# One core of attention and feed-forward: v staged in float32, w_out in long rows, transposes by head

## The chip, the cores and the metric

The kernel runs on one NeuronCore of a Trainium2 chip. The core has TensorE for matmuls (PE in the profile; PEld is its weight load), VectorE (DVE), ScalarE (ACT), GpSimd (POOL) and SyncE (SP), which work side by side and wait for one another by semaphores. SP and GpSimd issue most of the DMA transfers. The metric is the device time of one execution in microseconds (us); lower is better.

## The reference

Attention with a relative position bias is computed for 8 batches of 8 heads, 576 tokens, 64 values a head. Its output, 4608 tokens of 512 values, then goes through two dense layers with a leaky ReLU between.

```python
scores = q @ k.T / sqrt(64) + bias_table[bucket(|i - j|)]   # per batch and head, 576 x 576
attn   = softmax(scores)
x      = (attn @ v) -> 4608 x 512
h      = x @ w_in                       # 512 -> 2048
out    = maximum(0.01 * h, h) @ w_out   # 2048 -> 512
```

All inputs and the output are float32 in DRAM. The kernel works in bfloat16 inside.

## The kernel before

**Attention.** The heads are taken in pairs: 4 pairs a batch, 32 pairs in all, numbered 0 to 31. For a pair, q and k (96 rows of 6 x 64 values a head) are first brought into one row for both heads (`rows`, L385), transposed by TensorE into PSUM (`turn_by_pe`, L395) or, from pair 10, by DMA, and copied to SBUF as `qt` and `kt` (L407). `apart` (L411) adds a block in which the last 64 tokens of both heads stand apart. Six score units a pair follow (`score`, L432 to L440): units 0 to 3 each give 128 keys by 512 queries of both heads, units 4 and 5 the rest. ScalarE takes the exponential of each (L446, L448, L453) into the tile `at` (for pair 2 the tile `extra`), and VectorE multiplies the band near the diagonal by the exponential of the bias (`band`, L465), which comes from the tile `hk` (and `hk4` for the last 64 keys). `av` (L480, L482) multiplies with v, 25 matmuls a head; v lies in `vn` (512 tokens) and `v4` (the last 64), with a column of ones that gives the row sums. VectorE divides (L491, L492) into `opair`, and TensorE (L506, copied by VectorE at L510) or a DMA turns it into `xT`.

**Feed-forward.** Nine tiles T of 512 tokens. For each, 16 in-products of four matmuls (`ffn_in`, L523), each followed by a leaky ReLU on ScalarE (L528) into `gt`; then 4 groups of 16 matmuls (`ffn_out`, L535), a copy to SBUF (L540) and a store. Tile 0 needs the four pairs of batch 0; tile 1 needs batch 1 as well.

**Order.** The order of every engine is written by a planner (`Plan`): each step has an engine, a cost, the steps it needs and a rank; the planner plays them through and emits them in that order, so that on the chip every engine runs its list strictly in order. PSUM buffers are counted too (two for scores, one for `av`, a pool of three for the rest). While the plan is before its first feed-forward step, TensorE's planned idle time is filled with matmuls on a tile of zeros, `junk` (L712).

**Loads.** The float32 q and k of the first pair come by SP and ScalarE. GpSimd issues the loads that cast to bfloat16 on the way: q and k of the other pairs (L195, two or four heads a DMA), v of batch 1 (L225, L230) and later batches (L203, L209), the halves of w_in (L351) and of w_out (L357). The v of batch 0 is loaded by SP uncast into the tile `first` (L312, L314), behind the row of the bias (L308) and the loads of `hk` (L318, L325). GpSimd casts it into `vn` and `v4` (`cast_v`, L333, L336), after it has waited for all of it to issue the first half of w_in (`gate`, L339):

```python
pool_load(("w_in", 0), 1.0, lambda: (gate(vraw4[SL : SL + 1, 0, 0:1], SL), load_w_in(0)), WH, after=[vrt])
vc = [add("POOL", 0.6, [vrt] + prev, lambda c=c: cast_v(c), 0) for c in range(NJ + 1)]
```

The tile `first` shares two buffers of 16 KB a partition with `extra` and with the `gt` of the feed-forward tiles.

Of the kernel before, what the change touches and what calls it, by code (L numbers as in the profile page):

```python
# [36 lines left out]
class Plan:  # L37


    LAG = 0.25  # L40

    def __init__(self, slots):
        self.tasks = []
        self.slots = {k: [0.0] * v for k, v in slots.items()}

# [14 lines left out]
    def order(self):  # L60
# [4 lines left out]
        first = False  # L65
        while any(waiting.values()):
# [35 lines left out]
            if t["rank"] >= 10000 and e == "PE" and not first:  # L102
                first = True
                self.slots["M"].append(r)
                t["first"] = True
# [3 lines left out]
    def run(self, fill):  # L109

        fills = True
        for t in self.order():
            if t.get("first"):
                fills = False
# [8 lines left out]
def kernel(  # L123
# [17 lines left out]
    P = 128  # L141
# [72 lines left out]
    def load_v(b, h0, h1, by_head):  # L214
        i = b % NBUF
        p0, p1 = h0 // 2, h1 // 2
        if by_head:
            for h in range(h0, h1):
                nc.gpsimd.dma_start(
                    out=vn[i][:, :, h, 0:D],  # L220
                    in_=v[b, h, 0 : NJ * P, :].rearrange("(c s) d -> s c d", s=P),
                )
        else:
            for c in range(NJ):
                nc.gpsimd.dma_start(  # L225
                    out=vn[i][:, c, h0:h1, 0:D],
                    in_=v[b, h0:h1, c * P : (c + 1) * P, :].rearrange("h s d -> s h d"),
                )
        for e in range(2):
            nc.gpsimd.dma_start(  # L230
                out=v4[i][e * SL : (e + 1) * SL, p0:p1, e, 0:D],
                in_=v[b, h0 + e : h1 : 2, NJ * P : S, :].rearrange("h s d -> s h d"),
            )
# [18 lines left out]
    vraw_sb = first[:, qk_e : qk_e + NJ * H * D].rearrange("p (c h d) -> p c h d", c=NJ, h=H)  # L252
    vraw4 = first[:, qk_e + NJ * H * D : qk_e + (NJ * H + n_pairs) * D].rearrange("p (h d) -> p h d", h=n_pairs)
    extra = gt_pool.tile([P, n_fc, TT], BF16, name="extra", tag="gt").rearrange("p f t -> p (f t)")
    spare = extra[:, 0 : ATW + SL], extra[:, ATW + SL : ATW + SL + S + SL]
# [5 lines left out]
    load_qk(0, 2, 4)  # L261
    load_qk(0, 4, 6)
# [22 lines left out]
    clear_v(nc.gpsimd, 0)  # L285
    for i in range(3):
        clear_edges(nc.gpsimd, i)
    clear_v(nc.gpsimd, 1)
# [21 lines left out]
    def load_v_raw():  # L310
        for c in range(NJ):
            nc.sync.dma_start(out=vraw_sb[:, c, :, :], in_=v[0, :, c * P : (c + 1) * P, :].rearrange("h s d -> s h d"))  # L312
        for e in range(2):
            nc.sync.dma_start(out=vraw4[e * SL : (e + 1) * SL, :, :],  # L314
                                in_=v[0, e::2, NJ * P : S, :].rearrange("h s d -> s h d"))

# [13 lines left out]
    def cast_v(c):  # L330

        if c < NJ:
            nc.gpsimd.tensor_copy(out=vn[0][:, c, :, 0:D], in_=vraw_sb[:, c, :, :])  # L333
            return
        for e in range(2):
            nc.gpsimd.tensor_copy(out=v4[0][e * SL : (e + 1) * SL, :, e, 0:D], in_=vraw4[e * SL : (e + 1) * SL, :, :])  # L336

    def gate(t, row=0):
        nc.gpsimd.tensor_copy(out=w_in_sb[row : row + 1, 0, 0:1], in_=t)  # L339

# [11 lines left out]

    def load_w_out(half):
        if half > 1:
            return
        n = n_fc // 2
        nc.gpsimd.dma_start(  # L357
            out=w_out_sb[:, half * n : (half + 1) * n, :],
            in_=moe_w_out[half * n * P : (half + 1) * n * P, :].rearrange("(f p) e -> p f e", p=P),
        )  # L360


# [28 lines left out]

    def turn_by_pe(n, j):
        ps = turned[n, j] = ps_m_pool.tile([P, 8 * P], BF16, name="ps_t", tag="m")
        for c in range(NC):
            nc.tensor.transpose(ps[:, c * RQ : (c + 1) * RQ], in_=prs[n][0:RQ, j, c, :],  # L395
                                identity=ident[0:RQ, 0:RQ])
# [118 lines left out]
    def ffn_in(T, f0):  # L515
        t0, w = tiles[T]
        if f0 == 0:
            gts[T] = gt_pool.tile([P, n_fc, TT], BF16, name="gt", tag="gt")
        pm = pms[T, f0] = ps_m_pool.tile([P, TT], FP32, name="pm1", tag="m")
        for j in range(TT // w):  # L520
            f = f0 + j
            for c in range(n_cc):
                nc.tensor.matmul(pm[:, j * w : (j + 1) * w], lhsT=w_in_sb[:, c, f * P : (f + 1) * P],  # L523
                                 rhs=xT[c][:, t0 : t0 + w], start=(c == 0), stop=(c == n_cc - 1))

    def ffn_act(T, f0):
        t0, w = tiles[T]
        nc.scalar.activation(gts[T][:, f0 : f0 + TT // w, 0:w], pms.pop((T, f0)).rearrange("p (j t) -> p j t", t=w),  # L528
                             AF.Prelu, bias=0.0, scale=1.0, alpha=0.01)
# [17 lines left out]
    plan = Plan({"S": 2, "O": 1, "M": 2})  # L547
# [199 lines left out]
```

## Time and profile before

| | |
|---|---|
| median of 3 runs | 393.38 us (392.37 to 394.59) |
| the profiled execution | 393.96 us |
| its span in the trace | 392.2 us |
| TensorE busy | 376.5 us, 96% of the span |
| ScalarE, VectorE, GpSimd busy | 62%, 52%, 18% of the span |

The profiled execution lies 0.58 us above the median. Busy time on TensorE counts matmuls that overlap in the pipeline, so 96% is no proof that it runs at its peak; the chain that ended last, the waits of each engine and tables by stretch of time say more. A row of the timeline has the start, the duration, the engine, the line, the operation with its output and inputs, and a count; in brackets stands how long the engine was idle before it and who released it.

### The profile page before, as it was taken

The page shows a single profiled execution, that of the slowest core. Times are in us where ns is not written, and L with a number is a line of the kernel's source. Part 1 is how long each engine was busy: PE and PEld are TensorE (multiplying, and loading weights), DVE is VectorE, ACT ScalarE, POOL GpSimd, SP SyncE. Part 2 cuts the span into 40 slices and gives each one's busy share as a digit, 9 for nine tenths or more (in the row PEclk, how much of TensorE's full clock was granted, in tenths as well). Part 3 has the DMA queues.
Part 4 walks back from the last instruction along what each step waited for, and adds up shares of the span by engine and source line. Part 5 has one row for each costly group of instructions (what it writes and reads, how often), then busy time and mean ns, then how long its engine had stood idle before and what let it go on. Part 6 is the DMA issues. An engine that isn't in the chain of part 4 may idle for free.

```text
span 392.2 us, 8305 instructions
## 1 busy us (share of the span) xinstructions
PE 376.5 (96%) x3388; PEld 191.6 (49%) x3388; DVE 202.8 (52%) x539; ACT 243.6 (62%) x345; POOL 68.8 (18%) x112
## 2 busy tenths in 40 slices
PE   7849899999999999999999999999999999999995
PEld 2437355555455454545545555555555444444442
DVE  6637657886776666668567755555433201001021
ACT  3936689548966898688777766666675333333300
POOL 7267404043005201600700220000000000000000
PEclk8978999999999999999999999999999999999998
DMA  7969999779949984997995591111111010101012
GB/s 127 217 112 180 207 207 166 132 104 173 172 98 111 179 117 79 159 158 111 122 157 123 80 133 45 45 43 45 46 43 46 31 51 27 55 27 53 28 53 80
DMA packets 102741, 40.62 MB, mean 104 GB/s; under 512 B 81704, under 2 KB 97072, under 8 KB 102704
## 3 DMA queue, kind: packets, MB, share of 16 engines
q0 software_dynamic: 48512, 17.47, 40.8%
q1 hardware_dynamic: 53984, 22.33, 28.4%
q8 instruction: 26, 0.43, 0.4%
q10 hardware_dynamic: 208, 0.29, 0.3%
q14 instruction: 11, 0.09, 0.1%
HBM read 37.69 MB, written 9.45 MB: 120 GB/s over the span
## 4 chain that ended last, share of the span: by engine, by line
PE 89%; SPq 3%; DVE 2%; DMA 2%; ACT 1%; POOL 1%; issue 0%; DVEq 0%; POOLq 0%
PE pm L535 32%; PE pm L523 32%; PE ps_o L480 10%; PE ps_s L432 8%; PE ps_o L482 2%; SPq L312 2%; PE ps_s L436 2%; PE ps_s L439 2%; DMA tab<-in_bias_table_dram 1%; DMA first<-in_v_dram 1%; ACT at L446 1%; DVE opair L492 1%; POOL vn L333 1%; DVE at L465 1%; PE ps_t L395 0%; PE ps_om L480 0%
## 5 line engine op out<-in xcount | busy, mean ns | idle before, releaser
L523 PE MATMUL pm<-xT,w_in_sb 128*128 128x512 bf16 x576 | 145.0, 379 | 1.5 <-ACT gt L528 1.0
L535 PE MATMUL pm<-w_out_sb,gt 128*128 128x512 bf16 x576 | 143.3, 379 | 0.0
L446 ACT ACTIVATE at<-ps_s 128x1024 bf16<-128x1024 f32 x124 | 120.2, 1023 | 26.8 <-PE ps_s L432 25.6
L528 ACT ACTIVATE gt<-pm 128x512 bf16<-128x512 f32 x144 | 86.1, 601 | 75.4 <-PE pm L523 74.5
L535 PEld LDWEIGHTS <-gt 128*128 128x128 bf16 x576 | 52.7, 98 | 66.0 <-issue 8.9
L523 PEld LDWEIGHTS <-w_in_sb 128*128 128x128 bf16 x576 | 52.5, 98 | 64.2 <-issue 6.9
L465 DVE TENSOR_TENSOR at<-at,hk 128x768 bf16<-128x768 bf16 (+3 forms) x155 | 68.0, 453 | 24.5 <-ACT at L446 14.6
L540 DVE COPY y<-pm 128x512 f32<-128x512 f32 x36 | 24.8, 690 | 82.2 <-PE pm L535 81.7
L480 PEld LDWEIGHTS <-at 128*128 128x128 bf16 x1240 | 53.4, 99 | 22.2 <-issue 8.9
L480 PE MATMUL ps_o<-vn,at 128*128 128x65 bf16 x1180 | 54.7, 195 | 4.5 <-POOL vn L333 4.5
L482 PE MATMUL ps_o<-v,at 128*128 128x65 bf16 x295 | 48.1, 195 | 0.1
L203 POOL DMA_DIRECT2D vn<-in_v_dram x24 | 21.2, 896 | 136.3 <-PE ps_o L482 125.1
L432 PE MATMUL ps_s<-qt,kt 64*128 64x512 bf16 x256 | 40.7, 389 | 0.9 <-ACT at L453 0.3
L491 DVE RECIPROCAL rcp<-ps_o 128x5 f32<-128x5 f32 x60 | 11.7, 194 | 50.2 <-PE ps_o L482 50.0
L482 PEld LDWEIGHTS <-at 128*128 128x128 bf16 x310 | 30.7, 99 | 0.5 <-issue 0.5
L492 DVE TENSOR_TENSOR opair<-ps_o,rcp 128x320 bf16<-128x320 f32 x60 | 29.5, 492 | 2.3 <-DVE rcp L491 0.2
L448 ACT ACTIVATE at<-ps_s 128x512 bf16<-128x512 f32 x31 | 18.5, 598 | 12.1 <-PE ps_s L436 12.0
L407 DVE COPY qt<-tu 128x576 bf16<-128x576 bf16 x22 | 14.6, 666 | 14.8 <-PE ps_s L440 12.9
L453 ACT ACTIVATE at<-ps_s 128x576 bf16<-128x576 f32 x31 | 20.1, 649 | 0.0
L432 PEld LDWEIGHTS <-kt 64*128 64x128 bf16 x256 | 8.2, 94 | 20.8 <-issue 17.8
L407 DVE COPY kt<-tu 128x576 bf16<-128x576 bf16 x22 | 14.3, 652 | 0.0
L436 PEld LDWEIGHTS <-kt 128*128 128x128 bf16 x128 | 9.7, 99 | 6.9 <-ACT at L446 0.5
(77 smaller groups left out, 203.1 us busy)
## 6 DMA issues: line engine op xcount, KB each, us to landing
out_dram<-y SPq DMA_DIRECT2D x36, 256.0 KB, 2.1
qn<-in_q_dram POOLq DMA_DIRECT2D x14, 288.0 KB, 10.2
kn<-in_k_dram POOLq DMA_DIRECT2D x14, 288.0 KB, 11.5
vn<-in_v_dram POOLq DMA_DIRECT2D x28, 128.0 KB, 6.4
w_in_sb<-in_moe_w_in_dram POOLq DMA_DIRECT2D x2, 1024.0 KB, 9.5
w_out_sb<-in_moe_w_out_dram POOLq DMA_DIRECT2D x2, 1024.0 KB, 17.9
first<-in_v_dram SPq DMA_DIRECT2D x4, 256.0 KB, 7.0
hk<-u_row SPq DMA_DIRECT2D x1, 576.0 KB, 7.2
```

The source lines that it names most:

```text
L203: nc.gpsimd.dma_start(out=vn[i][:, c, :, 0:D], in_=v[b, :, c * P : (c + 1) * P, :].rearrange("h s d -> s h d"),)
L407: copy(out=t[:, 0:S].rearrange("p (r c) -> p r c", c=NC), in_=src)
L432: nc.tensor.matmul(ps[:, e, :], lhsT=kt[r, u * P : (u + 1) * P], rhs=qt[r, 0:512], start=True, stop=True)
L446: nc.scalar.activation(at[:, :, u, 0:512], ps, AF.Exp, scale=scale)
L465: nc.vector.tensor_tensor(out=o, in0=o, in1=m, op=ALU.mult)
L480: nc.tensor.matmul(ps[:, ic, :], lhsT=at[:, o : o + P], rhs=vn[i][:, c, 2 * p + e, :], start=(c == 0), stop=False)
L482: nc.tensor.matmul(ps[:, ic, :], lhsT=at4[:, ic * P : (ic + 1) * P], rhs=v4[i][:, p, e, :], start=False, stop=True)
L492: nc.vector.tensor_tensor(out=opairs[n][:, :, e * D : (e + 1) * D], in0=ps[:, :, 0:D], in1=rcp.to_broadcast([P, NJ + 1, D]), op=ALU.mult)
L523: nc.tensor.matmul(pm[:, j * w : (j + 1) * w], lhsT=w_in_sb[:, c, f * P : (f + 1) * P], rhs=xT[c][:, t0 : t0 + w], start=(c == 0), stop=(c ...
L528: nc.scalar.activation(gts[T][:, f0 : f0 + TT // w, 0:w], pms.pop((T, f0)).rearrange("p (j t) -> p j t", t=w), AF.Prelu, bias=0.0, scale=1 ...
L535: nc.tensor.matmul(ys[T, ts], lhsT=gts[T][:, f, ts * P : (ts + 1) * P], rhs=w_out_sb[:, f, :], start=(f == 0), stop=(f == n_fc - 1))
L540: nc.vector.tensor_copy(out=y, in_=ys[T, ts])
```

## The change

1. **v of batch 0** is no longer loaded by SP. GpSimd issues its loads, uncast, into `first`: heads 0 and 1 first (two DMAs of one head, two for the last 64 tokens), then heads 2 to 7 (four and two DMAs). GpSimd casts it in two steps, heads 0 and 1, then 2 to 7. Pair 0's `av` needs only the first step. The two `gate` copies are gone.
2. **v of batch 1** is loaded the same way into a third tile of the shared buffers (`staged`, in the place of `first`) and cast by GpSimd. The second half of batch 1's q and k and both halves of w_out are issued behind it.
3. **w_out** is loaded so that partition p holds 8 consecutive rows of a half, 8 KB in bfloat16. The hidden units of one in-product are then every eighth column of w_in (`hidden`), so the weights of L523 are read with a step of 8 elements.
4. **Pairs 1 to 4** are transposed head by head straight from `qn` and `kn`: 24 transposes of 96 x 64 in the place of 12 of 96 x 128 and of two row copies by VectorE.
5. **The first two in-products** of tile 0 are issued in two parts: three matmuls on pairs 0 to 2, and the fourth when pair 3 is there.
6. **Plan.** Other costs, ranks and slots; junk matmuls only up to the planned 26 us; GpSimd clears `v4` and `vn` of batch 0 ahead of its first load, and those of batch 1 later; `hk4` is loaded ahead of the larger part of `hk`; ScalarE copies the `qt` of pairs 5 to 7.

```diff
+        self.slots["M"][-1] = self.WARM
...
-            if fills and t["engine"] == "PE" and t["start"] > 6.0:
+            if t["engine"] == "PE" and 6.0 < t["start"] < self.WARM:
...
+    def stage_v(b, h0, h1):
+        m, t = stage_views(b)
+        if h1 - h0 < NJ:
             for h in range(h0, h1):
+                nc.gpsimd.dma_start(out=m[:, :, h, :], in_=v[b, h, 0 : NJ * P, :].rearrange("(c s) d -> s c d", s=P))
         else:
             for c in range(NJ):
+                nc.gpsimd.dma_start(out=m[:, c, h0:h1, :],
+                                    in_=v[b, h0:h1, c * P : (c + 1) * P, :].rearrange("h s d -> s h d"))
...
+    def cast_v(b, h0, h1):
+        m, t = stage_views(b)
+        nc.gpsimd.tensor_copy(out=vn[b][:, :, h0:h1, 0:D], in_=m[:, :, h0:h1, :])
...
-    def load_v_raw():
-        for c in range(NJ):
-            nc.sync.dma_start(out=vraw_sb[:, c, :, :], in_=v[0, :, c * P : (c + 1) * P, :].rearrange("h s d -> s h d"))
...
+            in_=moe_w_out[half * FH * P : (half + 1) * FH * P, :].rearrange("(p f) e -> p f e", f=FH),
...
+    def hidden(f):
+        o = (f // FH) * FH * P
+        return slice(o + f % FH, o + FH * P, FH)
...
+    def by_heads(n):
+        return 0 < n <= n_pairs
...
+                for e in range(2):
+                    nc.tensor.transpose(ps[e * D : (e + 1) * D, c * RQ : (c + 1) * RQ],
+                                        in_=(qn, kn)[j][b % NBUF][0:RQ, 2 * p + e, c, :], identity=ident[0:RQ, 0:RQ])
...
+            nc.tensor.matmul(pms[T, f], lhsT=w_in_sb[:, c, hidden(f)], rhs=xT[c][:, t0 : t0 + w],
+                             start=(c == 0), stop=(c == n_cc - 1))
...
-    plan = Plan({"S": 2, "O": 1, "M": 2})
+    plan = Plan({"S": 2, "O": 1, "M": 3})
...
+    pool_load(("qk", 0, 0), 1.4, lambda: load_qk(0, 2, 4), QK / 2, after=[dma(2.4)], rank=-9)
+    pool_load(("qk", 0, 1), 1.4, lambda: load_qk(0, 4, 6), QK / 2, rank=-9)
+    pool_load(("v", 0, 0), 2.8, lambda: stage_v(0, 0, 2), VS / 4 + 1.0, rank=-9)
+    edges = add("POOL", 1.0, list(prev), lambda: [clear_edges(nc.gpsimd, i) for i in range(3)], -8)
+    pool_load(("qk", 0, 2), 1.4, lambda: load_qk(0, 6, H), QK / 2 + 1.0, rank=-8)
+    pool_load(("v", 0, 1), 4.5, lambda: stage_v(0, 2, H), 3 * VS / 4 + 1.0, rank=-5)
+    pool_load(("qk", 1, 0), 1.4, lambda: load_qk(1, 0, 4), QK, rank=-4)
+    pool_load(("w_in", 0), 0.8, lambda: load_w_in(0), WH, after=[hkr], rank=-4)
+    vt[0] = [add("POOL", 1.2, [L["v", 0, 0]], lambda: cast_v(0, 0, 2), 5),
+             add("POOL", 2.4, [L["v", 0, 1]], lambda: cast_v(0, 2, H), 5)]
...
+        pool_load(("v", 1, 0), 5.0, lambda: (new_stage(), stage_v(1, 0, H)), VS, after=avt[2], rank=20)
+        pool_load(("qk", 1, 1), 1.4, lambda: load_qk(1, 4, H), QK, rank=20)
+        vt[1] = add("POOL", 3.2, [L["v", 1, 0]], lambda: cast_v(1, 0, H), 35)
...
+            if T == 0 and f < 2:
+                early = [add("PE", 0.65, [t for p in range(n_cc - 1) for t in nmt[p]] + w + xt[n_cc - 1][:f],
+                             lambda f=f: ffn_in(T, f, range(n_cc - 1)), rank - 3, take=["M"])]
```

The order that the planner writes for the changed kernel, as far as the prediction uses it. GpSimd: the identity; the clearing of batch 0's v tiles; q and k of pairs 1 and 2; v of heads 0 and 1; the edges; q and k of pair 3; `apart` for pair 1; v of heads 2 to 7; q and k of pairs 4 and 5; `apart` of pair 2's `kt`; the first half of w_in; `apart` of pair 2's `qt`; the two casts; the second half of w_in; the clearing for batch 1; v of batch 1; q and k of pairs 6 and 7; the cast; w_out. TensorE: three score units of pair 2, the first head of pair 0's `av`, a score unit, the second head, and so on. VectorE and ScalarE do the same steps as before around this, without the row copies of pairs 1 to 4. The first `av` of pair 4 stands behind 6 in-products (24 matmuls); before it stood behind 9.

More of the change, by code (lines that the diff above doesn't have):

```diff
@@ L101, in order @@
                 self.slots[k].append(t["end"] + self.LAG)
[L102 to L105, printed above, removed]
             done.append(t)
@@ L328, in load_hk4 @@
             )
[L330 to L339, printed above, removed]
     def mirrored(t, lo, hi):
@@ L651, in plan_pair @@
         sct[n] = ss
+        ext[n] = [es[NJ + 1]]
         cost = [0.43, 0.56, 0.56, 0.48, 0.25]
-        bt = [add("DVE", cost[c], [es[u] for u in ([c], [c], [c], [3, 4], [5])[c]] + [L["hk", 0 if n == 0 else 1]],
+        bt = [add("DVE", cost[c], [es[u] for u in ([c], [c], [c], [3, 4], [5])[c]] + [hk4t if c == NJ else L["hk", 0 if n == 0 else 1]],
                   lambda c=c: band(n, c), soon + 3) for c in range(NJ + 1)]
-        done = list(es.values()) + bt + [vt[b]]
+        done = list(es.values()) + bt + ([vt[b]] if b else [vt[0][min(p, 1)], edges])
         old = xt.get(n - 2, [])
@@ L700 @@
     for n in range(N):
+        if n == n_pairs:
+            late_loads()
         if n >= 2 * n_pairs and n % n_pairs == 0:
```

143 lines of the change are left out of this document (60 added, 83 removed).

## The prediction

> **What bounds the kernel now.** First the page: its busy row and its slices show how the span divides.
>
> ```profile
> PE 376.5 (96%) x3388; PEld 191.6 (49%) x3388; DVE 202.8 (52%) x539; ACT 243.6 (62%) x345; POOL 68.8 (18%) x112
> ...
> PEclk8978999999999999999999999999999999999998
> ...
> GB/s 127 217 112 180 207 207 166 132 104 173 172 98 111 179 117 79 159 158 111 122 157 123 80 133 45 45 43 45 46 43 46 31 51 27 55 27 53 28 53 80
> ```
>
> A slice is 9.8 us. The granted clock is low only in slices 0 to 3. So I read the chain of waits, in order of time (start, duration, what):
>
> ```profile
> 19.36 3.28 DMA first<-in_v_dram
> ...
> 24.11 2.28 POOL vn L333 x4
> ...
> 27.81 0.22 PE ps_o L480 x4
> ...
> 32.84 0.12 PE ps_om L480 x4
> ...
> 38.32 0.66 DVE pr L385
> ...
> 39.34 0.54 DVE pr L385 x2
> ...
> 41.90 0.86 PE pm L523 x4
> ...
> 43.35 1.94 ACT at L446 x2
> ...
> 53.14 0.12 PE ps_o L480 x4
> ...
> 373.35 14.69 PE pm L535 x68
> ```
>
> Until 26.8 us the end hangs on the transfer of batch 0's v and on GpSimd's casts of it. Then TensorE, ScalarE and VectorE take turns, and the first in-product starts at 41.90. The last stretch is 68 matmuls in 14.69 us, 0.216 us each, without a gap. The waits of each engine (total, times, longest) and stretches of time (length; busy time of PE, PEld, DVE, ACT, POOL; clock; DMA share; GB/s) show what v costs:
>
> ```profile
> PE ps_o L480 <- POOL vn L333: 4.5, 4, 3.5
> ...
> POOL w_in_sb L339 <- DMA first<-in_v_dram: 8.0, 1, 8.0
> ...
> ACT extra L446 <- PE ps_s L432: 6.0, 1, 6.0
> ```
>
> ```profile
> 20.00:25.00 5.00, 1.27 (x6) 0.54 (x6) 2.19 (x6) 2.67 (x3) 1.88 (x4) 0.99 0.33 46
> 25.00:30.00 5.00, 3.87 (x52) 3.00 (x52) 1.15 (x3) 1.02 (x1) 4.94 (x9) 0.50 0.99 174
> ...
> 60.00:80.00 20.00, 20.00 (x228) 11.02 (x225) 15.55 (x42) 13.62 (x19) 3.94 (x6) 1.00 1.36 136
> ```
>
> TensorE stands for most of 20 to 25 us, its clock is halved from 25 to 30, and ScalarE loses 6.0 us behind it, because pair 2's fourth score unit stands behind pair 0's `av` in TensorE's list. From 60 us on TensorE has no idle time. What the start saves should therefore reach the end, if nothing later runs late.
>
> **Part 1: when the first v is cast.** In the changed order GpSimd works almost without a pause, so its list sets this moment. The rows for it, and pair 1's `kt`, for which it waits once:
>
> ```profile
> 1.03 0.29 POOL masks.py:199 TENSOR_SCALAR_AFFINE_SELECT ident<-ident 128x128 bf16<-128x128 bf16 x1
> ...
> 4.13 0.57 POOL L236 MEMSET v<- 128x520 bf16 x1
> ...
> 5.59 0.16 POOL L244 MEMSET extra<- 128x64 bf16 x1
> ...
> 8.22 0.64 POOL L195 DMA_DIRECT2D kn<-in_k_dram  x1
> ...
> 10.47 0.76 DVE L407 COPY kt<-ps_t 128x576 bf16<-128x576 bf16 x1 [1.17 <-PE ps_t L395]
> 10.71 0.43 POOL L411 TENSOR_TENSOR qt<-qt,own 128x128 bf16<-128x128 bf16 x1 [1.85 <-ACT qt L407]
> ...
> 13.69 1.07 POOL L411 TENSOR_TENSOR kt<-kt,own 128x128 bf16<-128x128 bf16 x1 [0.18 <-DVE kt L407]
> ...
> 23.25 0.81 POOL L351 DMA_DIRECT2D w_in_sb<-in_moe_w_in_dram  x1 [0.30 <-POOL w_in_sb L339]
> ...
> 26.32 0.86 POOL L336 CAST v<-first 64x256 bf16<-64x256 f32 x2
> ...
> 28.45 3.53 POOL L225 DMA_DIRECT2D vn<-in_v_dram  x4
> 31.93 1.30 POOL L230 DMA_DIRECT2D v<-in_v_dram  x2
> ```
>
> The identity ends at 1.32. Clearing one v and the edges takes 4.13 to 5.75, 1.62 us. Eight issues for q and k cost 5.1 (0.64 each); of the ten for v, the four small ones cost 0.65 each and the six others between 0.65 and 0.88, together 7.1; w_in 0.81; four `apart` steps 1.7. Up to the one for pair 1 that is 9.6 us, while `kt` is ready at 11.23 as before (its loads leave 1.2 us later behind the clearing, but its two row copies are gone): a wait of 1.6. So 1.3 + 1.6 + 5.1 + 7.1 + 0.8 + 1.7 + 1.6 = 19.2, and with about 0.05 between 25 instructions 20.4. The first cast is one 512-element step of 0.57 (2.28 / 4) and two of at most 0.43; it ends at 21.3. The second is three times as much, 2.5 us: 24.0, if its data have landed. The last of them is issued near 17; 5.0 to 7.0 us from issue to landing (rows below) give 22 to 24, which moves the second cast's end to at most 26.5.
>
> The shortest `apart` is 0.43, the longest 1.07, beside VectorE's copies and bands. If the two casts (3.7 us) stretched likewise, the second would end near 29. I take no stretch: the 0.43 ran beside VectorE's `kt` copy (10.47 to 11.23). The 5 us stay for the range. [...]
>
> **Part 2: from there to tile 0.** More rows: ScalarE around its wait, the copy that completes `xT`, DMA issues (KB each, us to landing).
>
> ```profile
> 19.82 2.85 ACT L446 ACTIVATE extra<-ps_s 128x1024 bf16<-128x1024 f32 x3
> ...
> 28.68 1.02 ACT L446 ACTIVATE extra<-ps_s 128x1024 bf16<-128x1024 f32 x1 [6.00 <-PE ps_s L432]
> ...
> 41.68 0.46 DVE L510 COPY xT<-ps_tx 128x576 bf16<-128x576 bf16 x1
> ```
>
> ```profile
> w_out_sb<-in_moe_w_out_dram POOLq DMA_DIRECT2D x2, 1024.0 KB, 17.9
> ...
> first<-in_v_dram SPq DMA_DIRECT2D x4, 256.0 KB, 7.0
> ...
> qn<-in_q_dram POOLq DMA_DIRECT2D x3, 144.0 KB, 5.0
> ```
>
> Pair 0's first head takes five groups of 0.12 and about 0.03, 0.76 us, at full clock. So it ends at 22.1, and ScalarE goes on 0.6 later, the score between, at 22.7: just after its three exponentials (22.67), and 6.0 us earlier than 28.68. Between 28.68 and `xT` complete at 42.14 lie 13.46 us. Two things shorten them. The slow clock cost two heads of `av` 0.22 against 0.12 a group, about 1.1 in all. And of the three `pr` copies in the chain, 0.66 and half of 0.54 were pair 4's: 0.9. Pair 1 waits 0.3 longer for the second cast. That makes 11.8, and `xT` complete at 34.5: 7.7 us earlier.
>
> The early parts bring six matmuls of 0.216 forward into that wait, 1.3 us; the kernel before already had half of this (it started at 41.90, three matmuls ahead of its own copy), so 0.65 is new. The price is one PSUM buffer held longer, which is free then; without that cover an in-product waits, 0.86.
>
> **Part 3: what is late next.** v of batch 1 comes uncast behind pairs 4 and 5's q and k (576 KB in bfloat16) and all of w_in (2048 KB), on one queue. The page's slices show 180 to 217 GB/s while it is full. From 22 us, 2.6 MB at 200 take 13 us and v's 1.2 MB another 6: 41; the cast is 2.28 + 0.86 = 3.1, done at 44.1. At slice 1's 217 it is 42.6; I take 43.5. TensorE comes to pair 4's `av` 11.24 us after the first in-product in the kernel before (41.90 to 53.14); three in-products fewer lie between (2.6) and the early 1.3 are done, so 7.35 after 34.5, at 41.9. It waits 1.6 us, and as its list is in order the scores and in-products behind wait too. Bounds: 0, if the transfer moves like the casting loads did together; 5, if the uncast rows take twice my time. w_out leaves GpSimd behind that cast, near 44 to 46, and lands by 64 with the 17.9 of its row, against a first out-product (67.96 before) near 61: hidden if the queue is as empty as it should be by then, up to 3 if not; the 8 KB rows can only shorten this.
>
> **Part 4: the edits in TensorE's weights and lists.**
>
> ```profile
> L523 PEld LDWEIGHTS <-w_in_sb 128*128 128x128 bf16 x576 | 52.5, 98 | 64.2 <-issue 6.9
> ...
> L407 DVE COPY qt<-tu 128x576 bf16<-128x576 bf16 x22 | 14.6, 666 | 14.8 <-PE ps_s L440 12.9
> ...
> 44.11 0.68 PE L395 MATMUL ps_t<-ident,pr 96*128 96x96 bf16 x12
> 67.96 1.89 PE L535 MATMUL pm<-w_out_sb,gt 128*128 128x512 bf16 x8
> ```
>
> The strided weights: a load of 98 ns hides under a matmul of 216. No row has TensorE read with a step. The nearest is VectorE's copy from `tu`, which steps 192 bytes: 666 ns for 576 elements, 1.16 each. At that pace 128 columns take 148 ns: still hidden, nothing lost. It costs something only above 216; ends are 0 and whatever lies above, 576 times the excess. [...]
>
> Transposes by head: twelve took 0.68 with their latency; twice as many for pair 4 cost at most that again, and I take 0.3, since each fills half the columns; for pairs 1 to 3 they lie in idle time. `hk` later by the u row behind pair 0's copies: about 1 us, ahead of bands that `av` needs only after 21 us; uncovered, 1. The missing junk: TensorE is busy after 21 us; uncovered, the 0.50 clock again, some 2.5 us. `qt` of pairs 5 to 7 on ScalarE: takes 0.7 a pair off VectorE and puts it on an engine 62% busy; zero, at best a gain of one or two.
>
> **Sum.** 6.0 + 1.1 + 0.9 - 0.3 + 0.65 - 0.3 - 1.6 = 6.45 us. Against the profiled execution (393.96, span 392.2) that is 387.5; it stood 0.58 above the median, so 386.9 for the median, 1.6% less.
>
> **Rivals.**
> 1. The forecast, a gain of 4.5 to 9.5 (383.9 to 388.9): 0.58. More than that, if v lands and casts early, pair 4's wait is nothing and ScalarE's share in the chain at 43.35 (1.94) falls away too: 0.08.
> 2. A late v takes the place of the early one: GpSimd's casts stretch, or batch 1's v waits its 5 us. For it speaks that one engine and one queue now carry it all; against it the idle queue from 20 to 25 us (share 0.33). The gain shrinks below 4.5 us: 389 to 392.5. With the casts stretched by 5, 1.5 remains (391.9); with batch 1's v at 5 in the place of 1.6, 3.05 (390.3). 0.18, a third of it within half a per cent.
> 3. The change does not do what it says: GpSimd reaches the cast only at 25 to 26, because it must wait for slots of its earlier loads, and TensorE starts where it did. 393 give or take 1: 0.03.
> 4. Slower: the strided weights of L523. From 216 ns a load they set the pace; the start's gain is used up at 227 ns, since 576 x 11 ns is 6.5 us, and at 245 the time is 386.9 + 16.7 = 403.6. For it speaks that no row shows a stepped read by TensorE; against it the 148 ns by VectorE's pace, and that a load must take 2.3 times its 98 ns before it decides. 0.10. [...]
> 5. Slower by loads for batch 2 that now collide with w_out: 395 to 397, 0.03.
>
> **How the numbers follow.** Half a per cent, 2 us, is about what this measurement can tell from none. Faster: 0.58 + 0.08 + 0.12 = 0.78; same: 0.06 + 0.03 = 0.09; slower: 0.10 + 0.03 = 0.13. The range holds the forecast, rival 2, rival 3 in part and some of the larger gain: 383.0 to 392.5, about 0.8. Alone, the forecast's own is 383.9 to 388.9.
>
> **What will show it.** GpSimd's first cast of `vn` ends near 21.3, the second near 24; TensorE's wait for it falls from 4.5 to about 1; ScalarE's 6.0 is gone; the clock stays at 1.00 from 20 to 35; `xT` of pair 3 is complete near 34.5; a new wait of pair 4's `av` for GpSimd appears near 42; L523's weight loads stay below 216 ns and the last stretch at 0.216 a matmul. The prediction is wrong if GpSimd's list is late, if batch 1's v costs over 4 us, or if PEld on L523 grows past the matmul.

## The result

The changed kernel takes 397.74 us (median of 4 runs, 395.6 to 398.85). The kernel before took 393.44 beside it (4 runs). The ratio is 1.0102, with a 95% interval of 1.0063 to 1.014. The profiled execution took 397.54 us, with a span of 395.2. The forecast was 386.9, so 10.8 us are to be explained. Where executions of one kernel lie more than 1.5% apart, a ratio below counts only those within 1.5% of its fastest, while a median is that of all of them.

From the page: the busy row, the granted clock in 40 slices (9.9 us each here), and the weight loads of the first matmul.

```profile
PE 376.5 (95%) x3427; PEld 216.1 (55%) x3427; DVE 197.9 (50%) x528; ACT 244.7 (62%) x348; POOL 78.8 (20%) x123
...
PEclk9978999999899999999999999999999999999999
...
L509 PEld LDWEIGHTS <-w_in_sb 128*128 128x128 bf16 x576 | 79.2, 146 | 44.6 <-issue 4.9
```

The clock is low in slices 2 and 3, as before, and there is a new dip in slice 10, near 100 us. The chain of the changed kernel, in order of time (start, duration, what), has two long transfers in it:

```profile
8.28 2.43 DMA u_row<-ub
12.57 12.43 DMA hk<-u_row
25.10 1.93 DVE at L452 x5
...
86.22 11.71 DMA tu<-pr
101.00 0.96 PE ps_s L419 x3
...
376.56 14.69 PE pm L519 x68
```

The transfer of v, which stood at the head of this chain before, is gone from it. Its place has the transfer of `hk` for heads 2 to 7: it is issued at 12.57 and lands at 25.00, where the same load of the kernel before landed at 16.34 (issued 9.19, 7.15 us), and VectorE waited little for it. Two rows of the kernel before, from its page and from its waits:

```profile
hk<-u_row SPq DMA_DIRECT2D x1, 576.0 KB, 7.2
```

```profile
DVE at L465 <- DMA hk<-u_row: 1.4, 1, 1.4
```

The last stretch of the chain is as before, 14.69 us.

GpSimd's own list does what the change is about (its timeline; start, duration, and in brackets the idle time before and who ended it):

```profile
18.78 0.62 POOL L228 CAST vn<-first 128x512 bf16<-128x512 f32 x1
...
21.66 1.47 POOL L228 CAST vn<-first 128x1536 bf16<-128x1536 f32 x1 [1.74 <-DMA first<-in_v_dram]
23.07 0.75 POOL L231 CAST v<-first 64x192 bf16<-64x192 f32 x2
...
42.05 2.24 POOL L228 CAST vn<-staged 128x2048 bf16<-128x2048 f32 x1 [4.89 <-DMA staged<-in_v_dram]
```

The first cast of v is there at 19.9 and the second at 23.8. But the waits of the engines (total, times, longest) show who stands still now:

```profile
DVE at L452 <- DMA hk<-u_row: 9.8, 3, 3.8
...
PE ps_o L467 <- DVE opair L479: 9.1, 2, 6.3
...
ACT extra L440 <- PE ps_s L427: 7.7, 1, 7.7
...
DVE qt L394 <- DMA tu<-pr: 4.4, 1, 4.4
```

VectorE waits 9.8 us for `hk`. Its list is in order, so the division of pair 0 (`opair`) stands behind a band that waits for `hk`; TensorE's second head of pair 0 stands behind that division for 6.3 us, and ScalarE behind TensorE for 7.7. Before, ScalarE lost 6.0 here. Stretches of time (length; busy time of PE, PEld, DVE, ACT, POOL; clock; DMA share; GB/s):

```profile
20.00:25.00 5.00, 2.22 (x56) 1.76 (x54) 1.22 (x4) 2.83 (x4) 3.24 (x5) 1.00 1.24 208
25.00:30.00 5.00, 1.48 (x26) 1.48 (x27) 4.79 (x13) 0.00 (x0) 4.58 (x9) 0.54 1.13 213
30.00:35.00 5.00, 5.00 (x74) 3.21 (x72) 3.29 (x10) 3.26 (x4) 1.51 (x3) 0.78 1.10 246
...
95.00:100.00 5.00, 2.17 (x22) 1.30 (x19) 1.95 (x5) 2.47 (x4) 0.00 (x0) 1.00 1.36 170
100.00:105.00 5.00, 5.00 (x39) 2.42 (x39) 2.59 (x9) 2.70 (x4) 0.00 (x0) 0.66 1.47 130
```

The forecast was for pair 3's `xT`, complete at 34.5 instead of 42.14. Its copy in the changed kernel:

```profile
41.28 0.46 DVE L497 COPY xT<-ps_tx 128x576 bf16<-128x576 bf16 x1 [0.70 <-PE ps_tx L493]
```

It ends at 41.74: of the forecast 7.7 us, 0.4 are left. The first in-product starts at 40.1, 1.6 us earlier than before, because its first three matmuls are now issued as a part of their own, which does not need pair 3. And more than that is lost near 97 us, where TensorE stands again. First the kernel before there, in VectorE's timeline:

```profile
93.97 0.49 DVE L492 TENSOR_TENSOR opair<-ps_o,rcp 128x320 bf16<-128x320 f32 x1
97.67 0.65 DVE L407 COPY qt<-tu 128x576 bf16<-128x576 bf16 x1 [1.94 <-DMA tu<-pr]
```

Then the changed kernel, VectorE and TensorE:

```profile
98.02 0.64 DVE L394 COPY qt<-tu 128x576 bf16<-128x576 bf16 x1 [4.38 <-DMA tu<-pr]
...
99.35 0.49 DVE L479 TENSOR_TENSOR opair<-ps_o,rcp 128x320 bf16<-128x320 f32 x1
...
99.90 0.30 PE L467 MATMUL ps_o<-vn,at 128*128 128x65 bf16 x4 [2.83 <-DVE opair L479]
```

The transposing DMA was late before too: issued at 88.26, landed at 97.58, 9.3 us. There the division stood ahead of the copy that waited for it. The changed plan puts the copy first, so the wait reaches TensorE.

### The profile page after: what moved, and what is told of

The parts are those of the page before. It is cut to its first block, busy times and chain, and to the rows that moved or that the text cites. A ratio compares the mean times of both kernels' runs of the same rounds, so it can differ in the third digit from the quotient of the medians.

```text
span 395.2 us, 8382 instructions
## 1 busy us (share of the span) xinstructions
PE 376.5 (95%) x3427; PEld 216.1 (55%) x3427; DVE 197.9 (50%) x528; ACT 244.7 (62%) x348; POOL 78.8 (20%) x123
## 4 chain that ended last, share of the span: by engine, by line
PE 87%; DMA 8%; DVE 2%; ACT 1%; SPq 0%; issue 0%; DVEq 0%; ACTq 0%
PE pm L519 32%; PE pm L509 30%; PE ps_o L467 9%; PE ps_s L419 8%; DMA hk<-u_row 3%; DMA tu<-pr 3%; PE ps_o L469 2%; PE ps_s L426 2%; PE ps_s L423 2%; DMA first<-in_k_dram 1%; PE ps_t L377 1%; DMA u_row<-ub 1%; DVE at L452 1%; PE ps_om L467 1%; PE ps_tx L493 1%; ACT at L433 0%
## 5 line engine op out<-in xcount | busy, mean ns | idle before, releaser
L509 PE MATMUL pm<-xT,w_in_sb 128*128 128x512 bf16 x576 | 148.4, 384 | 0.0
L509 PEld LDWEIGHTS <-w_in_sb 128*128 128x128 bf16 x576 | 79.2, 146 | 44.6 <-issue 4.9
L519 PEld LDWEIGHTS <-gt 128*128 128x128 bf16 x576 | 51.9, 98 | 63.2 <-issue 11.0
L452 DVE TENSOR_TENSOR at<-at,hk 128x768 bf16<-128x768 bf16 (+3 forms) x155 | 67.7, 453 | 31.6 <-ACT at L433 12.4
L467 PEld LDWEIGHTS <-at 128*128 128x128 bf16 x1240 | 52.6, 99 | 25.7 <-DVE opair L479 9.7
L467 PE MATMUL ps_o<-vn,at 128*128 128x65 bf16 x1180 | 53.8, 195 | 9.1 <-DVE opair L479 9.1
L196 POOL DMA_DIRECT2D vn<-in_v_dram x24 | 22.2, 937 | 133.2 <-PE ps_o L469 125.2
L478 DVE RECIPROCAL rcp<-ps_o 128x5 f32<-128x5 f32 x60 | 11.7, 195 | 44.4 <-PE ps_o L469 44.0
L469 PEld LDWEIGHTS <-at 128*128 128x128 bf16 x310 | 30.5, 98 | 0.5 <-ACT at L440 0.5
L394 DVE COPY kt<-tu 128x576 bf16<-128x576 bf16 x22 | 15.3, 695 | 0.0
L426 PE MATMUL ps_s<-qt,kt 128*128 128x512 bf16 x32 | 12.4, 387 | 1.2 <-ACT at L433 1.2
## 6 DMA issues: line engine op xcount, KB each, us to landing
kn<-in_k_dram POOLq DMA_DIRECT2D x14, 288.0 KB, 10.7
w_out_sb<-in_moe_w_out_dram POOLq DMA_DIRECT2D x2, 1024.0 KB, 10.9
```

What stands on the lines that cost most here:

```text
L196: nc.gpsimd.dma_start(out=vn[i][:, c, :, 0:D], in_=v[b, :, c * P : (c + 1) * P, :].rearrange("h s d -> s h d"),)
L394: copy(out=t[:, 0:S].rearrange("p (r c) -> p r c", c=NC), in_=src)
L452: nc.vector.tensor_tensor(out=o, in0=o, in1=m, op=ALU.mult)
L467: nc.tensor.matmul(ps[:, ic, :], lhsT=at[:, o : o + P], rhs=vn[i][:, c, 2 * p + e, :], start=(c == 0), stop=False)
L469: nc.tensor.matmul(ps[:, ic, :], lhsT=at4[:, ic * P : (ic + 1) * P], rhs=v4[i][:, p, e, :], start=False, stop=True)
L509: nc.tensor.matmul(pms[T, f], lhsT=w_in_sb[:, c, hidden(f)], rhs=xT[c][:, t0 : t0 + w], start=(c == 0), stop=(c == n_cc - 1))
```

## The experiments

Theory A in the expectations is this, or what the expectation itself says: the late `hk` takes the gain of the start, the wait at 97 us takes more, and the stepped weights take the rest. Each run is beside runs of the kernel before on the same chip.

### The three suspects, one at a time

**Without the late `hk`.**

```diff
-            m = mirrored(hk[:, 2 * p : 2 * p + 2, :], lo - (c - 1) * P, hi - (c - 1) * P)
+            m = mirrored(hk[:, 0:2, :], lo - (c - 1) * P, hi - (c - 1) * P)
...
-    hkr = add("SP", 0.1, [urt], lambda: load_hk(2, H), 1, tail=7.2)
+    hkr = add("SP", 0.1, [urt], lambda: None, 1, tail=7.2)
```

> The changed kernel, without the load of hk for heads 2 to 7; all pairs take the band of heads 0 and 1, so the bias of pairs 1 to 3 of every batch is another one. Same order on every engine. Theory A (the late hk ate the gain of the start): VectorE's 9.8 us of waiting for hk falls below 4, pair 0's av stays at about 20 us and pair 1's follows at 24, the first in-product starts near 35 in place of 40.2, and the time falls by 3 to 5 us (393 to 395). Rival B (the start is held by GpSimd's casts and by batch 1's v whatever hk does): the first in-product moves by less than 2, or the gain is lost again at pair 4's av waiting for the cast of batch 1's v (45.4 us in the changed kernel), and the time falls by less than 2.

Measured: 392.06 us (10 runs, 388.7 to 397.21), 5.7 us less than the changed kernel. The ratio to before, 0.9943 (0.9917 to 0.9969), counts the seven runs up to 393.33. The first in-product starts at 35.4. The order of the lists is the same, so having this load in the start costs about 5.7 us. The run leaves the load out, and not only its lateness; without it the last of v for heads 2 to 7 lands earlier too (20.99 against 22.15, though issued 1.2 us later). So 5.7 is an upper bound for what the lateness alone costs. The waits of this run show that the loss at the transposes is still there, and as large:

```profile
DVE qt L394 <- DMA tu<-pr: 5.0, 1, 5.0
...
PE ps_o L467 <- DVE opair L479: 3.5, 1, 3.5
```

**The transposing DMA counted as 12 us in the plan, not 6.**

```diff
-            d = add("SP", 0.1, [r0, r1] + cut.get(n - 4, [])[:2], lambda: turn_by_dma(n), rank, tail=6.0)
+            d = add("SP", 0.1, [r0, r1] + cut.get(n - 4, [])[:2], lambda: turn_by_dma(n), rank, tail=12.0)
```

> The changed kernel with one number of the planner changed: a transposing DMA of q and k is planned to take 12 us in place of 6, so the copies from tu stand later in VectorE's list. Theory A (the loss near 97 us comes from VectorE's list standing on a late transpose): VectorE's 4.4 us and TensorE's 2.8 us of waiting there are gone, the clock stays at 1.00 from 100 to 105 us, and the time falls by 3 to 5 us. Rival B (whatever the order, the transposes are as late as the loads make them): a like wait stands elsewhere and the time stays within 1 us.

Measured: 394.01 us (10 runs), ratio 1.0008 (0.9992 to 1.0024): 3.7 us less than the changed kernel (whose four runs spread from 395.6 to 398.85). Nothing but the order of the lists has changed, over the whole kernel. The wait for `hk` stands (8.6 us), the one near 97 is gone, and the clock stays up there:

```profile
95.00:100.00 5.00, 4.95 (x68) 3.38 (x68) 3.34 (x10) 4.72 (x7) 0.00 (x0) 1.00 1.47 172
100.00:105.00 5.00, 4.95 (x50) 3.17 (x50) 3.56 (x12) 4.64 (x9) 0.00 (x0) 1.00 0.90 176
```

**Part 3 undone: weights and rows of w_out as before.**

```diff
-            in_=moe_w_out[half * FH * P : (half + 1) * FH * P, :].rearrange("(p f) e -> p f e", f=FH),
+            in_=moe_w_out[half * FH * P : (half + 1) * FH * P, :].rearrange("(f p) e -> p f e", p=P),
...
-        o = (f // FH) * FH * P
-        return slice(o + f % FH, o + FH * P, FH)
+        return slice(f * P, (f + 1) * P)
```

> The changed kernel with part 3 undone: w_out in the old rows, the weights of the in-products contiguous. Same order on every engine. Theory A (the stepped weights cost a little each): the weight load of the in-products goes from 146 ns back to 98, their mean distance from 222 back to 216 ns, and the time falls by 2 to 3.5 us. Rival B (the load stays hidden under the 216 ns of the matmul, as forecast): within 0.5 us of the changed kernel. Rival C (the long rows of w_out matter): slower by 1 or more, because w_out lands late.

Measured: 396.48 us (6 runs, 394.08 to 398.33), ratio 1.0079 (1.0049 to 1.0109): 1.3 us less than the changed kernel by the medians. That is less than expected, and not clear of the spread, since the two intervals overlap. The traces, read under "Part 3 alone" below, put a like figure on it. Its weight loads:

```profile
L508 PEld LDWEIGHTS <-w_in_sb 128*128 128x128 bf16 x576 | 52.9, 98 | 61.8 <-issue 3.5 <-DMA qn<-in_q_dram 0.4
```

**All three together.** The edits are the three above.

> The changed kernel with all three suspects taken away: hk of heads 2 to 7 is not loaded (every pair uses the band of heads 0 and 1, so the bias of the other heads is left out), the plan counts 12 us for a transposing DMA, and part 3 is undone (weights and w_out rows as before). Theory A (the three are the whole loss and add up): 397.7 - 5.6 - 3.7 - 1.3 = 387.1, between 386 and 389, near the forecast of 386.9; TensorE's wait for opair at 99 us is gone. Rival (they overlap, or something else in the lists takes back what the start gains): 390 to 393.

Measured: 386.42 us (6 runs), ratio 0.9856 (0.9818 to 0.9893), 11.3 us less than the changed kernel; the single steps add up to 10.7. As in the first run, the load of `hk` for heads 2 to 7 is left out altogether. The clock is 1.00 in every stretch from 10 to 105 us, and the first in-product starts at 35.2. TensorE's longest wait in the whole run is this:

```profile
PE ps_o L466 <- DVE opair L478: 1.3, 1, 1.3
```

So the three together account for the 10.8 us, within the spread of the runs. That the time agrees with the forecast of 386.9 to half a us is in part luck. Pair 3's `xT` is complete at 36.79, not at 34.5:

```profile
36.33 0.46 DVE L496 COPY xT<-ps_tx 128x576 bf16<-128x576 bf16 x1 [0.65 <-PE ps_tx L492]
```

These 2.3 us are made up for elsewhere, 1.6 of them by the wait that the forecast had for pair 4's `av`. It was not paid, as TensorE comes to it at 43.19 and the cast of batch 1's v ends at 43.2. The parts that held, such as the row copies and the early in-products, were not tried one by one.

### Part 3 alone, in the kernel before

```diff
-            in_=moe_w_out[half * n * P : (half + 1) * n * P, :].rearrange("(f p) e -> p f e", p=P),
+            in_=moe_w_out[half * n * P : (half + 1) * n * P, :].rearrange("(p f) e -> p f e", f=n),
...
-                nc.tensor.matmul(pm[:, j * w : (j + 1) * w], lhsT=w_in_sb[:, c, f * P : (f + 1) * P],
+                nc.tensor.matmul(pm[:, j * w : (j + 1) * w], lhsT=w_in_sb[:, c, hidden(f)],
```

> The kernel before with part 3 alone: w_out loaded in 8 KB rows, and the first matmuls reading their weights with a step of 8 elements. Theory A (the steps cost 1.3 us, as undoing them in the changed kernel gave): weight loads 146 ns instead of 98, time 393.5 + 1.3 = 394.8, between 393.9 and 395.8. Rival (no cost, the weight load being hidden under 216 ns of matmul as predicted; the 1.3 us came from elsewhere): 393.0 to 393.8. A gain from the longer rows would show as less than 393.

Measured: 398.68 us (6 runs) against 393.22, ratio 1.0137 (1.0112 to 1.0161): 5.5 us, four times the 1.3 that was expected. TensorE's list is the same, instruction for instruction, so the two traces can be set beside each other load by load. The profiled execution (397.55, the fastest of the six) falls back 2.4 us between 40 and 44, and another 1.9 between 44 and 300, a little in every tile. The first piece is a wait that the kernel before does not have (waits of this run):

```profile
PE ps_o L485 <- POOL vn L333: 4.4, 4, 3.3
PE pm L528 <- DMA w_in_sb<-in_moe_w_in_dram: 2.1, 1, 2.1
```

It stands before the second weight load of the first in-product, which the trace starts at 43.58, just behind the landing of the second half of w_in (43.53), though these weights lie in the first half:

```profile
43.58 0.42 PEld L528 LDWEIGHTS <-w_in_sb 128*128 128x128 bf16 x3 [2.42 <-DMA w_in_sb<-in_moe_w_in_dram]
```

In the kernel before that half lands at 44.19, and all four loads start before it:

```profile
41.70 0.57 PEld L523 LDWEIGHTS <-w_in_sb 128*128 128x128 bf16 x4
```

In the changed kernel that half lands at 36.17, ahead of the first in-product at 40.1, and nothing is lost by it. The second piece is the stepped load itself: in 50 of the 139 in-products after 50 us, the third weight load comes some 241 instead of 216 ns behind the second; in the kernel before, in none. The changed kernel has 44 such of 136, about 1.1 us in all at 25 ns each. The other 1.2 us of the 5.5 are not seen in this profile, whose execution took 1.1 less than the median. The step and the 8 KB rows of w_out were not tried apart.

### Why `hk` was late

**`hk` of heads 2 to 7 by GpSimd, ahead of v.**

```diff
-    def load_hk(h0, h1):
-        nc.sync.dma_start(
+    def load_hk(h0, h1, eng=nc.sync):
+        eng.dma_start(
...
-    hkr = add("SP", 0.1, [urt], lambda: load_hk(2, H), 1, tail=7.2)
...
+    hkr = pool_load(("hk", 1), 0.7, lambda: load_hk(2, H, nc.gpsimd), 3.0, after=[urt], rank=-7)
```

> The changed kernel with hk for heads 2 to 7 issued by GpSimd, ahead of v of heads 2 to 7 on the same queue, in place of by SP. Theory A (two queues share the DMA engines, and SP's small rows starve beside GpSimd's loads): hk lands by 17 us in place of 25.0, the casts of heads 2 to 7 end near 25, the first in-product starts near 36 and the time falls by 2 to 4 us. Rival B (the load of hk is slow by its own rows): it lands after 20 us again, v is late too, and the time rises by 0 to 3.

Measured: 395.52 us (5 runs, 393.54 to 398.75), ratio 1.0043 (1.0015 to 1.0071). The fall of 2.2 us is within the 2 to 4 of Theory A, but the landing agrees with neither theory: `hk` is issued at 10.89 and lands at 19.01, 8.1 us, in the profiled execution, the slowest of the five. VectorE's wait for it falls to 4.1; but v is later behind it, and TensorE now waits 2.1 us for GpSimd's cast of `vn`. Another 2.0 the profile puts down to GpSimd's clearing of batch 1's `vn`, which the `av` doesn't need; VectorE's division ends at the same moment.

**Everything of GpSimd's held until `hk` is there.**

```diff
+    def gate():
+        nc.gpsimd.tensor_copy(out=stage_views(0)[0][0:1, 0, 2, 0:1], in_=hk[0:1, 2, 0:1])
-    pool_load(("v", 0, 1), 4.5, lambda: stage_v(0, 2, H), 3 * VS / 4 + 1.0, rank=-5)
+    pool_load(("v", 0, 1), 4.5, lambda: (gate(), stage_v(0, 2, H)), 3 * VS / 4 + 1.0, after=[hkr], rank=-5)
```

> The changed kernel with one added step: before GpSimd loads v of batch 0's heads 2 to 7, it copies one element of hk of heads 2 to 7 into the place where v will land, so that this v and all of GpSimd's loads behind it leave only when hk is there. Theory A (the 12.43 us come from sharing the DMA engines with GpSimd's loads): hk takes 5.5 to 7.5 us, as in the kernel before (7.15), and lands at 18 to 20; v of heads 2 to 7 lands near 28 and is cast near 30, TensorE waits for that instead, and the time is 396 to 400. Rival (hk is slow by itself, its 768 rows of 768 bytes or the hk4 loads ahead of it): it still takes 10 us or more, and the time is 401 or more.

Measured: 397.27 us (2 runs). The DMA view gives size and time to landing; the changed kernel's row first, then that of this run:

```profile
hk<-u_row SPq DMA_DIRECT2D x1, 576.0 KB, 12.4
```

```profile
hk<-u_row SPq DMA_DIRECT2D x1, 576.0 KB, 5.4
```

It is issued at 12.65, as late as in the changed kernel (12.57) and behind the same `hk4` loads, and takes less than half the time. What makes the difference, then, is whether v and GpSimd's loads behind it run beside it. Of the lateness (8.7 us against the kernel before) 3.4 are the later issue and 5.3 the longer flight in that company. The time, 397.27, is no better, since v itself is now late, as Theory A expected.

**The u row first, and `hk` ahead of `hk4`.**

```diff
-    L["raw", 0], L["raw", 1], tabl = dma(4.3), dma(4.6), dma(5.0)
+    L["raw", 0], L["raw", 1], tabl = dma(4.3), dma(4.6), dma(3.8)
...
-    hk4t = add("SP", 0.1, [urt], load_hk4, 0, tail=5.0)
-    hkr = add("SP", 0.1, [urt], lambda: load_hk(2, H), 1, tail=7.2)
+    hkr = add("SP", 0.1, [urt], lambda: load_hk(2, H), 0, tail=7.2)
+    hk4t = add("SP", 0.1, [urt], load_hk4, 1, tail=5.0)
```

> The changed kernel with the u row copied by VectorE ahead of pair 0's kt copy (the table planned at 3.8 us instead of 5.0), and SP loading hk of heads 2 to 7 ahead of hk4. Theory A (hk is late because it was moved behind pair 0's copies and behind the hk4 loads, and because its rows then share the DMA engines with v of heads 2 to 7): hk of heads 2 to 7 is issued near 10.3 instead of 12.57 and takes 8 to 10 us, landing at 18.5 to 20.5 instead of 25.0; VectorE's wait for hk falls from 9.8 us to 4 to 5, and the time is 394.5 to 396. Rival (the 12.43 us of this load hang on something that the place in SP's list doesn't change): it lands at 22.5 or later, and the time is 397 or more.

Measured: 398.11 us (4 runs), ratio 1.0096 (1.0058 to 1.0134): no gain. The profiled execution is the slowest of the four, 399.76:

```profile
hk<-u_row SPq DMA_DIRECT2D x1, 576.0 KB, 6.8
...
hk<-u_row SPq DMA_DIRECT2D x2, 96.0 KB, 10.9
```

`hk` lands at 17.61, sooner than Theory A expected; the time is in the rival's range. What is late is the second `hk4` load: it is issued at 12.09, 0.74 us behind GpSimd's first load of v (11.35), and lands at 24.32. VectorE waits 10.4 us for `hk` and `hk4`, 7.1 at once. In both orders the SP load that leaves last, behind the start of v, is the late one: 12.4 us from issue to landing there, 12.2 here. The wait near 97 stands here too.

### A version that beats both

**Early `hk`, 12 us for a transposing DMA, part 3 undone**, all as in the diffs above:

> The run with the early u row and hk ahead of hk4, and with 12 us counted for a transposing DMA and part 3 undone: nothing of the computation is left out. Theory A: what the early hk gives (2 to 3 us) and 3.7 and 1.3 add up: 397.7 - 2.5 - 5.0 = 390.2, between 389 and 392, faster than the kernel before by 0.4 to 1.1%. Rival (hk stays late): 392.5 to 394, no faster than before.

Measured: 11 runs from 387.03 to 394.12, median 393.16, no faster than the kernel before (393.37 beside it), within the rival's range. The ratio, 0.9918 (0.9883 to 0.9954), counts only the four runs up to 392.05. In the profiled execution, the fastest, GpSimd's first load of v left at 12.44, behind the last `hk4` load (11.93), and `hk4` landed at 18.01. Half a us lies between the two. The seven runs above 393 left no trace; that v left ahead of `hk4` in them is a guess, which the next run puts to the test.

**The same, with v held until `hk` of heads 0 and 1 is there.**

```diff
+    def gate():
+        nc.gpsimd.tensor_copy(out=stage_views(0)[0][0:1, 0, 2, 0:1], in_=hk[0:1, 0, 0:1])
-    pool_load(("v", 0, 1), 4.5, lambda: stage_v(0, 2, H), 3 * VS / 4 + 1.0, rank=-5)
+    pool_load(("v", 0, 1), 4.5, lambda: (gate(), stage_v(0, 2, H)), 3 * VS / 4 + 1.0, after=[hkt, hk4t], rank=-5)
```

> The run with early u row, hk ahead of hk4, 12 us for a transposing DMA and part 3 undone, and one added step: GpSimd copies one element of hk of heads 0 and 1 into the place of v of heads 2 to 7 before it loads that v. So this v always leaves behind all of SP's hk loads (near 14.3 us), not 1 us before or after them as chance has it. Nothing of the computation is left out. Theory A (the spread of the run without this step, 387 to 394, and the granted clock of 1.00 to 0.98 that goes with it, come from whether v's first load is issued ahead of hk4 or behind it): hk and hk4 land by 18.5, the times lie closer together, and the median is 387 to 390.5. Rival (v is then itself too late, cast near 27, and TensorE waits for it and loses its clock): 391 to 394.

Measured: 389.85 us (12 runs, eleven of them from 389.28 to 391.46, one at 394.13), ratio 0.9925 (0.9901 to 0.995): faster than both kernels, by 0.75% and 2.0%, and 2.9 us above the forecast. With v held, the runs lie much closer together, which supports the guess. v now leaves at 15.24, `hk` takes 5.6 us, `hk4` lands at 19.05. One wait remains in the start: the plan has put pair 0's `av` ahead of ready scores, and TensorE stands 2.5 us for the band that needs `hk4`.

**Only the start mended** (the early u row and `hk`, and the same gate; the rest as in the change):

> The changed kernel with only the start mended: early u row, hk ahead of hk4, and v of heads 2 to 7 held until hk of heads 0 and 1 is there; the transposing DMA counted as 6 us and part 3 as in the change. Theory A (the lateness of hk costs 5.5 us however it is taken away): hk and hk4 land by 18.5 and the time is 391 to 394, near the 392.1 of the run without hk of heads 2 to 7. Rival: 396 or more, as in the run with the early hk alone (398.1).

Measured: 391.54 us (10 runs), ratio 0.996 (0.9939 to 0.9981): 6.2 us less than the changed kernel, as expected, and near the 392.06 of the run without the late `hk`. But that agreement is in part luck. Part 3 and the short count for the DMA are still in it, yet the wait near 97 is gone, since the changed start leads to another order there. The fair neighbour is the run with 12 us for the DMA (394.01), which has no wait near 97 either, and part 3 too: against it the mended start is worth 2.5 us. TensorE still waits 2.1 us in this start, and the clock is half for 6.8. Undoing part 3 and counting 12 us as well brought 1.7 us more, to the 389.85 above.

**Real times for the bias in the plan.**

```diff
-    urt = add("SP", 0.1, [cpu], store_u_row, -1, tail=1.5)
+    urt = add("SP", 0.1, [cpu], store_u_row, -1, tail=3.0)
...
-    hk4t = add("SP", 0.1, [urt], load_hk4, 1, tail=5.0)
+    hk4t = add("SP", 0.1, [urt], load_hk4, 1, tail=8.5)
...
-    pool_load(("v", 0, 1), 4.5, lambda: (gate(), stage_v(0, 2, H)), 3 * VS / 4 + 1.0, after=[hkt, hk4t], rank=-5)
+    pool_load(("v", 0, 1), 4.5, lambda: (gate(), stage_v(0, 2, H)), 3 * VS / 4 + 1.0, after=[hkt], rank=-5)
```

The edit also takes `hk4` out of what v waits for in the plan.

> The run with all of the start mended, and the plan given the times that its trace shows for the bias: 3.0 us for storing the u row instead of 1.5, 8.5 for hk4 instead of 5.0 (hk4 landed at 19.05 there, 6.6 us after its issue, and TensorE stood 2.5 us at 17 to 19.5 for the band that needs it, since the plan had put pair 0's av ahead of other scores). Nothing of the computation is left out. Theory A (a plan with too short a tail puts a waiting step ahead of work that is ready): the scores of pair 1 go ahead of pair 0's av, TensorE's wait of 2.5 us at 19 and the half clock behind it are gone, and the median is 386.5 to 388.5. Rival (the wait only moves): 389.5 or more, as in the run without this edit (389.85).

Measured: 391.64 us (6 runs), ratio 0.9948 (0.9931 to 0.9965). The rival held: the wait for `hk4` is gone, and TensorE stands 3.8 us for GpSimd's cast in its place, in two waits. The median is 1.8 us above that of the run without this edit.

## Why the prediction was wrong

**The failed step is one sentence of part 4:** "`hk` later by the u row behind pair 0's copies: about 1 us, ahead of bands that `av` needs only after 21 us; uncovered, 1". It counted only the issue, and even that was 3.4 us later, not 1: 0.85 by the u row's own place (8.28 against 7.43), 1.15 by its slower store (why that is slower stays open), and 1.4 by the two `hk4` loads put ahead. It did not ask what would run beside the transfer: GpSimd, which in the kernel before issued no load between 8.9 and 23.25 us, now issues v of heads 2 to 7 from 10.68 on, then q and k, and w_in from 17.59. `hk` landed at 25.00, 8.7 us later than before. Uncovered, it cost up to 5.7 us, not 1: that is what leaving the load out took back. With the load kept and the start mended, 2.5 were won.

**A step is missing:** what is late after batch 0. The sum let the gain of the start run through to the end, "if nothing later runs late". It never looked at the transposing DMAs, late in the trace of before by 1.94 us of VectorE's time, and covered there by nothing but the order of VectorE's list. The plan counts them as 6 us where two of them took 9.3 (before) and 11.7 (changed) around 90 us. A changed start gives another order, and 3.7 us were lost. Rival 5 names a time near the result (395 to 397), but not this mechanism: the largest part of the loss is in the start, and most of the rest came by the order of a list.

**A term was mis-sized:** the stepped weights, at "hidden, nothing lost". The estimate of 148 ns a load was right (146), and so was that 146 is under 216. But a mean under 216 did not hide every load; that the step costs something only above 216 was an estimate of part 4, and the runs don't show it. In 44 of 136 in-products of the changed kernel the third load came some 25 ns late, and in the kernel before with part 3 TensorE waited 2.1 us at the landing of the other half of w_in. It cost some 1.1 to 1.3 us here, the first by the trace and the second by medians that are not clear of the spread, and with the 8 KB rows 5.5 in the kernel before, 2.1 of it that wait. With the step a load took 146 ns, without it 98.

**What held.** GpSimd's list: the second cast ended at 23.8, forecast 24.0; the first at 19.9, forecast 21.3. The 5 us of stretch that the range allowed for the casts did not come, but the changed kernel can't show it: VectorE stood idle for `hk` while the second cast ran (21.66 to 23.82). In the run without the late `hk` bands ran all through it, and the cast took 0.6 us longer in all:

```profile
20.72 1.52 POOL L228 CAST vn<-first 128x1536 bf16<-128x1536 f32 x1 [0.23 <-DMA first<-in_v_dram]
22.18 1.29 POOL L231 CAST v<-first 64x192 bf16<-64x192 f32 x2
```

Batch 1's v was cast by 45.5, 2 us later than forecast, and TensorE, which came later still, did not wait for it; w_out was hidden, its halves landing 10.9 us after their issue with the 8 KB rows, 11.4 with the old rows (part 3 undone) and 17.9 in the kernel before. And the sum as a total: without the three, 386.42 us, against 386.9, though two of its terms were off there, `xT` 2.3 us later and the wait of 1.6 absent, and so partly by luck.

## What to carry to other kernels

When a change moves loads to another queue or to an earlier time, list every transfer that will be in flight beside them, and look for the one whose landing ends a wait; a duration from the old trace may not hold in new company, as the 576 KB of `hk` took 7.15 us in the kernel before and 12.43 beside v. A stall that is covered only by the order of one engine's list is a debt: price it whenever a planner will write that list again. And before trusting a plan's order, compare its durations with those of the trace. Setting the transposing DMA's won 3.7 us here; setting those of the bias only moved a wait.

## What the runs showed of the hardware

**Half clock came in multiples of 3.4 us.** In twelve of the fourteen profiles there are, in the first 120 us, stretches of half clock between two at full clock, and each lasts 3.4, 6.8, 10.2 or 13.6 us, within 0.1 a multiple of 3.4; those at the very start of a span are left out here, and what lies behind 120 us. In the rows of the changed kernel above, (1 - 0.54) x 5 + (1 - 0.78) x 5 = 3.4 us of clock are missing between 25 and 35, so 6.8 us ran at half, and 3.4 us (0.34 x 5 / 0.5) near 100. The run with only the start mended:

```profile
15.00:20.00 5.00, 2.57 (x30) 1.60 (x31) 2.39 (x7) 1.30 (x3) 5.00 (x7) 0.58 0.72 172
20.00:25.00 5.00, 4.83 (x67) 3.18 (x66) 3.64 (x9) 3.92 (x5) 4.49 (x7) 0.74 1.06 170
```

gives 6.8 again. Both stretches of the changed kernel come behind a stand of TensorE: it was busy for 2.22 of the 5 us from 20 to 25, and for 2.17 of those from 95 to 100. Such a stall cost itself, and then about 1.7 us of work for each 3.4 at half: in the kernel before, the groups of `av` follow one another every 0.27 us at half clock (near 27 us) and every 0.15 at full (near 33). The stall was not always long: in this last run TensorE's longest wait was 2.1 us, in a stretch where it was busy for 2.57 of 5 us. Nor did the length alone decide: in the run without the late `hk` a wait of 2.3 us, in a stretch with 2.99 of 5 us busy, cost no clock. What does is not shown.

**Loads by SP that left behind the start of v landed late.** The 576 KB of `hk` took 5.4 us with v held back, 8.1 on GpSimd's queue ahead of v, and 12.4 by SP when they left 1.9 us behind the first load of v for heads 2 to 7; and two loads of 96 KB took 10.9 on average when the second left 0.74 us behind it.

**The stepped weight load was not free under a longer matmul.** At 146 ns, under a matmul of 216, it still delayed about a third of the in-products (44 of 136 in the changed kernel, 50 of 139 in the kernel before with part 3), by some 25 ns each; at 98 ns, without the step, none in the kernel before.
